# One load per chunk of keys, a product ahead of warming, second weights issued by ACT, decoding steps moved into the loop

## The chip, the cores and the metric

The kernel runs on one core of one Trainium2 chip. The metric is the device time in microseconds of one execution. The engines are PE (matrix products), DVE, ACT and POOL (elementwise work); SP only issues DMAs. SP, ACT and POOL each issue DMAs from their own instruction stream: an issue that waits holds up every instruction behind it on that engine.

## The reference

Three layers, one behind the other, on 2 sequences of 768 tokens, all in float32:

```python
for t in range(S):                                  # delta rule, 2 x 8 heads of 48
    y[:, :, t] = einsum('bhd,bhde->bhe', q[:, :, t], state)
    v_old = einsum('bhde,bhd->bhe', state, k_n[:, :, t])
    state += b[t] * outer(k_n[:, :, t], v[:, :, t] - v_old)
...
e = argmax(logits) if s == 0 or local_gate < 0.5 else previous e      # 8 experts, 384 -> 1024 -> 384
out[b, s] = p[e] * (relu(x[b, s] @ w1[e]) @ w2[e])
...
h = relu(x @ w_in); gate = sigmoid(conv over 3 tokens of h); result = (h * gate) @ w_out
```

## The kernel before, in words

**Attention.** The tokens are cut into 12 chunks of 64, six pairs of chunks. For each chunk `load_kq,c` brings keys and queries into rows 0 to 47 (heads of the first half) and 64 to 111 (second half) of one tile; rows 48 to 63 stay unused. `gram,c` multiplies keys with keys and queries on PE into one of two PSUM tiles `g`, `gev,c` (ACT, line 406) and `mev,c` (DVE, line 401) copy the result out, after which the next `gram` may use that tile. For each pair a triangular system is solved in steps `d,g,j` (lines 555 and 557; `g` numbers the system, and chunks 0 and 1 are system 0, 2 and 3 are system 1, while chunks 4 to 7 make the wide system 2, steps `dw`). System 0 is solved on POOL, behind `n5,0` (line 540), which needs `n3,0` on DVE and so stands behind `gev,5` on ACT and `mev,5` on DVE; system 1 is solved on DVE. `x2,0` (line 567) on DVE follows on the last step of system 0 and, in DVE's order, on `d,1,0`. The products `pp`, `jt`, `m1`, `m2` then build the pair's inverse; `ipv` (line 611) copies the product of `pp` out. `warm,s,n` are `n` products whose result nobody reads. The whole order is one string of words, `ORDER`; each engine takes its own instructions of it in that order.

**Experts.** At the end of attention the routing (`route1` to `route4`) finds each token's slot, POOL scatters the rows to the DRAM tensor `xs` (line 231), and `place` builds the first expert's input on PE (line 245). `Moe.start` loads the first expert's weights in four pieces (`load(0, 0..3)`: two of `w1`, two of `w2`, 768 KB each), `conv` splits a piece into two parts (ACT line 822, DVE line 823), and `split` does so for the input (ACT line 922). Each expert then runs 72 products `ph` (line 886) and 48 products `py` (line 903). From the second expert on, its input comes from `xs` by the load `xe` (line 835) and is transposed on PE (line 847).

**Last layer.** `moe2` runs 16 steps (sequence, block of 128 columns). `gemm1` (line 1096) is copied out by ACT (line 1097), `conv` (lines 1103 to 1105), `gate` and `gsplit` alternate between ACT and DVE, and `gemm2` (line 1130) sums up. `extra()` is one decoding step of the last two blocks of `w_out` (lines 996 to 1006), which `gemm2` needs only in steps 6 and 7. The loop over the steps begins after a ramp in which six steps' `gemm1` have been started.

DMAs that SP and ACT issue signal on eight semaphores, `DMAHW0` to `DMAHW7`; an issue waits until the DMA that used its semaphore before has landed.

Of the kernel before, what the change touches and what calls it, by code (L numbers as in the profile page):

```python
# [18 lines left out]
D = 48  # L19
# [259 lines left out]
class Attention:  # L279
# [76 lines left out]

    def load_kq(self, c):
        self.KQ[c] = self.kqp.tile([128, 2, 4, 2, 64], F32, name="kq", tag="kq", k=c)
        for e in range(2):
            (self.nc.scalar if e and c < 8 else self.nc.sync).dma_start(out=self.KQ[c][64 * e:64 * e + D], in_=self.kq[c, e])  # L360

    def load_v(self, p):
        self.V[p] = self.natp.tile([128, 2, 8, DV], F32, name="vn", tag="vn", k=p)
# [6 lines left out]
    def load_c(self):  # L370
        self.nc.scalar.dma_start(out=self.bt, in_=self.beta)
        self.nc.scalar.dma_start(out=self.btw, in_=self.betaw)
        self.nc.sync.dma_start(out=self.wgt, in_=self.wgb)

    def load_vt(self, p):
        self.VT[p] = self.vtp.tile([96, 2, 4, 128], F32, name="vt", tag="vt", k=p)
# [343 lines left out]
    def my(self, c, s):  # L720
        y = self.g[s][:, :, 0:4 * DV].rearrange("p e (i n) -> p e i n", i=4)
        for i in range(4):
# [4 lines left out]
                                          start=(c == 0 and i == 0), stop=True, skip_group_check=True)  # L727


ORDER = ("load_kq,0 load_kq,1 consts load_kq,4 load_kq,5 load_kq,2 load_kq,3 load_kq,6 load_c load_kq,7 load_k,0 "  # L730
# [41 lines left out]
def attention(A, R, ys):  # L772
# [4 lines left out]
                  r4=lambda k, s: R.route4(k, A.bank(s)), hot=lambda c, e: R.hot(A.gp, c, e), place=lambda c: R.place(A.sps, c), rc=R.consts, cx=R.clear_x, cy=lambda k: R.clear_y(ys, k))  # L777
    for w in ORDER.split():
        n, *a = w.split(",")
# [3 lines left out]
class Moe:  # L783
# [13 lines left out]
        self.pp = pool("m_p", 2)  # L797
        self.R, self.W, self.X, self.H = {}, {}, {}, {}

    def load(self, e, k):  # L800

        if e >= NE:
            return
        t = self.raw.tile([128, 1536], F32, name="raw", tag="raw")
        if k < 2:
            v = t.rearrange("p (k f) -> p k f", k=3)
            self.nc.sync.dma_start(out=v, in_=self.w1[e, :, 512 * k:512 * k + 512].rearrange("(k p) f -> p k f", p=128))
        else:
            g = k - 2
            v = t.rearrange("p (k d) -> p k d", k=4)  # L810
            self.nc.sync.dma_start(out=v, in_=self.w2[e, 512 * g:512 * g + 512, :].rearrange("(k p) d -> p k d", p=128))
        self.R[e, k] = v

    def conv(self, e, k):
        if e >= NE:
            return
        nc = self.nc
        p, sh = (self.w1p, [128, 3, 512]) if k < 2 else (self.w2p, [128, 4, DM])
        h = p.tile(sh, F32R, name="wh", tag="wh")
        l = p.tile(sh, F32R, name="wl", tag="wl")  # L820
        r = self.R.pop((e, k))
        nc.scalar.copy(out=h, in_=r)  # L822
        nc.vector.tensor_tensor(out=l, in0=r, in1=h.bitcast(F32), op=ALU.subtract)  # L823
        self.W[e, k] = (h, l)
        self.load(e + 1, k)
# [97 lines left out]
            self.nc.vector.tensor_tensor(out=l[:, c], in0=p, in1=h[:, c].bitcast(F32), op=ALU.subtract)  # L923

    def start(self, ctx, w, done):
        for k in range(2):
            self.load(0, k)
        for k in range(2, 4):
            self.load(0, k)
        self.conv(0, 0)  # L930
        self.split(w)
        for e in (1, 0):
            self.loadx(e)
        self.conv(0, 1)
        done()
        self.pt, self.ph, self.py = (ctx.enter_context(self.tc.tile_pool(name=n, bufs=k, space=PSUM)) for n, k in (("m_pt", 2), ("m_ph", 3), ("m_py", 3)))
        self.trx(0)
# [108 lines left out]
def moe2(ctx, tc, W, ys, idn, out, wm, decode):  # L1046
    nc = tc.nc
# [3 lines left out]
    extra = lambda: next(dec, None) if dec else None  # L1051
# [7 lines left out]
    def bank():  # L1059

        if ramp:
            p, t = ramp.pop(0)
            ramp.append((p, t))
        else:
            p, t = pa, "npt"
        return p.tile([128, 384], F32, name=t, tag=t)
# [5 lines left out]
    def xtr(b, tb):  # L1072
        if tb == 0:
            XT[b] = [xp.tile([128, 3, S], F32R, name=f"nx{b}{j}") for j in range(2)]
        x = XR.pop((b, tb))
        p = bank().rearrange("p (k t) -> p k t", k=3)
        for k in range(3):
            nc.tensor.transpose(out=p[:, k], in_=x[:, 128 * k:128 * k + 128], identity=idn)
        h, l = XT[b]
        s = slice(128 * tb, 128 * tb + 128)  # L1080
        nc.scalar.copy(out=h[:, :, s], in_=p)
        nc.vector.tensor_tensor(out=l[:, :, s], in0=p, in1=h[:, :, s].bitcast(F32), op=ALU.subtract)

    def gemm1(b, f, c, n=2):

        if c == 0:
            H[b, f] = HB[(8 * b + f) % 7]
        h = H[b, f]
        wh, wl = W["inn"]
        xh, xl = XT[b]  # L1090
        fs = slice(128 * f, 128 * f + 128)
        w = S // n
        p = bank()[:, 0:w]
        cs = slice(w * c, w * c + w)
        for j, (k, (a, x)) in enumerate((k, ax) for k in range(3) for ax in ((wh, xh), (wh, xl), (wl, xh))):
            nc.tensor.matmul(out=p, lhsT=a[:, k, fs], rhs=x[:, k, cs], start=(j == 0), stop=(j == 8))  # L1096
        nc.scalar.activation(out=h[:, 1 + w * c:1 + w + w * c], in_=p, func=AF.Relu)  # L1097

    def conv(b, f):
        h = H[b, f]  # L1100
        c = C[b, f] = hp.tile([128, S], F32, name="nc", tag="nc", bufs=5)
        cw = W["conv"]
        nc.scalar.activation(out=c, in_=h[:, 0:S], func=AF.Copy, scale=cw[:, f, 0:1])
        nc.vector.scalar_tensor_tensor(out=c, in0=h[:, 1:S + 1], scalar=cw[:, f, 1:2], in1=c, op0=ALU.mult, op1=ALU.add)
        nc.vector.scalar_tensor_tensor(out=c, in0=h[:, 2:S + 2], scalar=cw[:, f, 2:3], in1=c, op0=ALU.mult, op1=ALU.add)

    def gate(b, f):
        h, c = H.pop((b, f)), C.pop((b, f))
        nc.scalar.activation(out=c, in_=c, func=AF.Sigmoid)  # L1109
        nc.vector.tensor_tensor(out=c, in0=c, in1=h[:, 1:S + 1], op=ALU.mult)  # L1110
        G[b, f] = c

    def gsplit(b, f):
        c = G.pop((b, f))
        gh = hp.tile([128, S], F32R, name="ngh", tag="ngh", bufs=3)
        gl = hp.tile([128, S], F32R, name="ngl", tag="ngl", bufs=3)
        nc.scalar.copy(out=gh, in_=c)
        nc.vector.tensor_tensor(out=gl, in0=c, in1=gh.bitcast(F32), op=ALU.subtract)
        GT[b, f] = (gh, gl)

    def gemm2(b, f):
        if f == 0:
            for t in range(6):
                O[b, t] = po.tile([128, DM], F32, name=f"no{t}", tag=f"no{t}")
        gh, gl = GT.pop((b, f))
        wh, wl = W["out"]
        for t in range(6):
            ts = slice(128 * t, 128 * t + 128)
            for j, (a, w) in enumerate(((gh, wh), (gl, wh), (gh, wl))):
                nc.tensor.matmul(out=O[b, t], lhsT=a[:, ts], rhs=w[:, f], start=(f == 0 and j == 0), stop=(f == 7 and j == 2))  # L1130

    def fin(b):
        for t in range(6):
            o = hp.tile([128, DM], F32, name="nout", tag="nout", bufs=6)
            (nc.scalar.copy if t % 2 == 0 else nc.vector.tensor_copy)(out=o, in_=O.pop((b, t)))
            r0 = b * S + t * 128
            nc.sync.dma_start(out=out[r0:r0 + 128, :], in_=o)
# [17 lines left out]
    for c in range(2):  # L1155
        for f in range(3):
# [2 lines left out]
                xtr(0, 2 * c + f + 2)  # L1159
            if (c, f) == (0, 1):  # L1160
                extra()
    extra()
    extra()
    extra()
    gemm1(0, 0, 2, 3)
    conv(0, 0)
    gemm1(0, 1, 2, 3)
    gemm1(0, 2, 2, 3)
    gemm1(0, 3, 0)
    xtr(1, 0)  # L1170
    gate(0, 0)
    conv(0, 1)
    gemm1(0, 3, 1)
    xtr(1, 1)
# [8 lines left out]
    for i, s in enumerate(steps):  # L1183
        near, far = (steps[i + n] if i + n < len(steps) else None for n in (2, 5))
        if far:
            gemm1(*far, 0)
        if near:
            gate(*near)
        if i + 1 < len(steps):
            gsplit(*steps[i + 1])  # L1190
        if far:
            gemm1(*far, 1)
        if i in (1, 2):
            xtr(1, i + 2)
        if i + 4 < len(steps):
            conv(*steps[i + 4])
        gemm2(*s)
        if i == 2:
            xtr(1, 5)
        if s[1] == 7:  # L1200
            fin(s[0])

# [148 lines left out]
```

## Time and profile before

| | |
|---|---|
| time, median of 3 runs | 455.54 us (454.3 to 455.74) |
| the profiled execution's own time | 458.59 us |
| its span in the profile | 456.9 us |
| PE busy | 397.1 us (87%) |
| DVE, ACT, POOL busy | 296.7, 203.5, 125.0 us |
| chain that ended last, by engine | PE 74%, DVE 10%, ACT 5%, issue 4%, DMA 4% |
| mean granted TensorE clock | 0.886 of full speed |

The profiled execution is 3.05 us above the median of the runs, and its span is 1.7 us below its time. The three layers lie at about 0 to 188 us, 188 to 337 us and 337 to 457 us.

### The profile page before, as it was taken

To read this page: it belongs to the slowest core of one execution; us is meant where nothing else is said; L and a number is where in the kernel's file an instruction comes from. 1 tells how busy PE (TensorE), PEld (TensorE's weight loads), DVE (VectorE), ACT (ScalarE), POOL (GpSimd) and SP (SyncE) were. 2 spreads that over 40 slices of the span, in tenths; PEclk is the share of its full clock that TensorE was granted. 3 is DMA by queue.
4 is the path that set the end of the run, shared out by engine and by line. 5 is a ranking of instruction groups with operands and counts; after the bars stand their busy time and mean duration, and the time that the engine had idled before them with its cause. 6 is when DMAs were issued, how large, how long until landed. Compare 5 with 4: busy or idle time off the path is not lost.

```text
span 456.9 us, 13270 instructions
## 1 busy us (share of the span) xinstructions
PE 397.1 (87%) x5779; PEld 359.9 (79%) x5802; DVE 296.7 (65%) x532; ACT 203.5 (45%) x344; POOL 125.0 (27%) x260
## 2 busy tenths in 40 slices
PE   5676658868769688899999999999999799999994
PEld 3633347647657567789999999999979799999993
DVE  2666982561563115489777999999916976567671
ACT  1531221634422122177564665665435846446641
POOL 7073888482710802402022021120220000000000
PEclk9577865985986579799999999999999999999997
DMA  8949482530101215769968876972054000002003
GB/s 199 230 153 324 148 278 80 141 114 4 39 4 38 109 37 180 235 211 335 382 228 302 262 266 241 292 260 107 36 162 150 1 0 1 0 2 103 1 1 110
DMA packets 34273, 65.84 MB, mean 144 GB/s; under 512 B 3392, under 2 KB 21664, under 8 KB 34208
## 3 DMA queue, kind: packets, MB, share of 16 engines
q1 hardware_dynamic: 31040, 56.90, 39.3%
q0 software_dynamic: 1792, 5.56, 3.1%
q10 hardware_dynamic: 1376, 2.46, 2.2%
q8 instruction: 47, 0.77, 0.7%
q14 instruction: 18, 0.15, 0.1%
HBM read 49.05 MB, written 15.86 MB: 142 GB/s over the span
## 4 chain that ended last, share of the span: by engine, by line
PE 74%; DVE 10%; ACT 5%; issue 4%; DMA 4%; SPq 0%; ACTq 0%; DVEq 0%
PE ph L886 15%; PE py L903 15%; PE no L1130 11%; PE npt L1096 8%; PE sps L245 3%; PE g L352 3%; DMA kq<-in_kq_dram 2%; DMA xs<-zt 2%; PE W L671 2%; PE g L619 2%; PE g L643 2%; PE g L658 1%; DVE X L557 1%; DVE tm L555 1%; PE g L726 1%
## 5 line engine op out<-in xcount | busy, mean ns | idle before, releaser
L823 DVE TENSOR_TENSOR wl<-raw,wh 128x1536 fp32r<-128x1536 f32 x32 | 56.1, 1753 | 4.3 <-ACT wh L822 3.5
L915 POOL DMA_INDIRECT ys<-y,oi x16 | 25.8, 1613 | 119.8 <-ACT y L912 114.4
L886 PE MATMUL ph<-xh,wh 128*128 128x256 f32 x192 | 54.7, 285 | 0.8 <-ACT xh L922 0.8
L886 PE MATMUL ph<-xl,wh 128*128 128x256 f32 x192 | 54.4, 283 | 0.2 <-DVE xl L923 0.2
L886 PE MATMUL ph<-xh,wl 128*128 128x256 f32 x192 | 54.4, 283 | 0.0
L1130 PE MATMUL no<-wout,ngh 128*128 128x384 f32 x192 | 51.5, 340 | 0.0
L822 ACT CAST wh<-raw 128x1536 fp32r<-128x1536 f32 x32 | 47.2, 1475 | 0.3 <-DMA raw<-in_w_dram 0.3
L1096 PE MATMUL npt<-nx,win 128*128 128x384 f32 (+1 forms) x225 | 42.2, 340 | 2.5 <-ACT nh L1097 2.5
L903 PE MATMUL py<-wh,hh 128*128 128x384 f32 x128 | 43.6, 341 | 0.0
L903 PE MATMUL py<-wh,hl 128*128 128x384 f32 x128 | 43.1, 337 | 0.0
L903 PE MATMUL py<-wl,hh 128*128 128x384 f32 x128 | 43.0, 336 | 0.0
L1096 PEld LDWEIGHTS npt<-nx,win 128*128 128x128 f32 x225 | 39.4, 193 | 3.1 <-ACT nh L1097 2.8
L886 PEld LDWEIGHTS ph<-xh,wh 128*128 128x128 f32 x192 | 36.8, 192 | 1.5 <-ACT xh L922 1.3
L886 PEld LDWEIGHTS ph<-xl,wh 128*128 128x128 f32 x192 | 36.8, 192 | 0.4 <-DVE xl L923 0.4
L886 PEld LDWEIGHTS ph<-xh,wl 128*128 128x128 f32 x192 | 36.8, 192 | 0.0
L1130 PEld LDWEIGHTS no<-wout,ngh 128*128 128x128 f32 x192 | 35.2, 188 | 0.0
L1130 PE MATMUL no<-wout,ngl 128*128 128x384 f32 x96 | 32.5, 339 | 0.0
L352 PE MATMUL g<-wm 128*128 128x512 bf16 x65 | 25.8, 500 | 5.4 <-issue 1.5
L1110 DVE TENSOR_TENSOR nc<-nc,nh 128x768 f32<-128x768 f32 x16 | 15.3, 957 | 21.0 <-ACT nc L1109 21.0
L386 PE MATMUL g<-kq 48*64 48x128 f32 x192 | 17.8, 335 | 8.7 <-DVE M L401 8.7
L1097 ACT ACTIVATE nh<-npt 128x384 f32<-128x384 f32 (+1 forms) x25 | 12.0, 485 | 29.9 <-PE npt L1096 29.9
L903 PEld LDWEIGHTS py<-wh,hl 128*128 128x128 f32 x128 | 24.1, 188 | 0.3 <-DVE hl L890 0.3
(234 smaller groups left out, 882.3 us busy)
## 6 DMA issues: line engine op xcount, KB each, us to landing
raw<-in_w_dram SPq DMA_DIRECT2D x32, 768.0 KB, 6.8
xs<-zt SPq DMA_DIRECT2D x4, 786.0 KB, 14.1
kq<-in_kq_dram SPq DMA_DIRECT2D x16, 192.0 KB, 5.0
raw<-in_win_dram SPq DMA_DIRECT2D x6, 512.0 KB, 6.9
raw<-in_wout_dram SPq DMA_DIRECT2D x8, 384.0 KB, 6.0
xe<-xs SPq DMA_DIRECT2D x7, 393.0 KB, 6.2
vn<-in_vn_dram SPq DMA_DIRECT2D x6, 456.0 KB
kn<-in_kn_dram SPq DMA_DIRECT2D x6, 384.0 KB
```

The source lines that it names most:

```text
L245: self.nc.tensor.matmul(out=w[:, b, HCAP * k:HCAP * k + HCAP], lhsT=self.x[r, c // 2, c % 2, 128 * k:128 * k + 128], rhs=self.OH[c // 8][r ...
L352: self.nc.tensor.matmul(out=w, lhsT=self.wm[:, 0:128], rhs=self.wm, start=True, stop=True)
L386: mm(out=t[r, 0, i].rearrange("p w t -> p (w t)"), lhsT=k[:, 0], rhs=k.rearrange("p w t -> p (w t)"), start=True, stop=True)
L822: nc.scalar.copy(out=h, in_=r)
L823: nc.vector.tensor_tensor(out=l, in0=r, in1=h.bitcast(F32), op=ALU.subtract)
L886: nc.tensor.matmul(out=p[:, j].rearrange("p (c t) -> p c t", c=2), lhsT=a[:, k, fs], rhs=c[:, k], start=(n == 0), stop=(n == 8))
L903: nc.tensor.matmul(out=self.Y[c], lhsT=a[:, j, ts], rhs=w[:, f], start=(f2 == 0 and j == 0 and n == 0), stop=(f2 == 3 and j == 1 and n == 2))
L915: nc.gpsimd.indirect_dma_start(out=self.views[c][e], out_offset=bass.IndirectOffsetOnAxis(ap=I[:, c:c + 1].bitcast(U32), axis=0), in_=y, i ...
L1096: nc.tensor.matmul(out=p, lhsT=a[:, k, fs], rhs=x[:, k, cs], start=(j == 0), stop=(j == 8))
L1097: nc.scalar.activation(out=h[:, 1 + w * c:1 + w + w * c], in_=p, func=AF.Relu)
L1110: nc.vector.tensor_tensor(out=c, in0=c, in1=h[:, 1:S + 1], op=ALU.mult)
L1130: nc.tensor.matmul(out=O[b, t], lhsT=a[:, ts], rhs=w[:, f], start=(f == 0 and j == 0), stop=(f == 7 and j == 2))
```

## The change

Four edits:

1. Keys and queries of a chunk come in one load of 112 rows (0 to 111), which writes zeros into rows 48 to 63; 448 KB in place of two loads of 192 KB. All are issued by SP, where ACT issued the second half of chunks 0 to 7. The three small loads of `load_c` are all issued by ACT, first of all.
2. `ipv,0` is written directly behind `pp,0` in `ORDER`, ahead of five warming products that write the same PSUM tile.
3. The two `w2` pieces of the first expert are issued by ACT, behind ACT's half of the first `conv`; they were issued by SP directly behind the `w1` pieces.
4. Three decoding steps, ahead of the last third of `gemm1` in the ramp, go behind steps 1, 2 and 3 of the loop.

```diff
     def load_kq(self, c):
-        for e in range(2):
-            (self.nc.scalar if e and c < 8 else self.nc.sync).dma_start(out=self.KQ[c][64 * e:64 * e + D], in_=self.kq[c, e])
+        self.nc.sync.dma_start(out=self.KQ[c][0:64 + D], in_=self.kq[c])
...
-        self.nc.sync.dma_start(out=self.wgt, in_=self.wgb)
+        self.nc.scalar.dma_start(out=self.wgt, in_=self.wgb)
...
-ORDER = ("load_kq,0 load_kq,1 consts load_kq,4 load_kq,5 load_kq,2 load_kq,3 load_kq,6 load_c load_kq,7 load_k,0 "
+ORDER = ("load_kq,0 load_c load_kq,1 consts load_kq,4 load_kq,5 load_kq,2 load_kq,3 load_kq,6 load_kq,7 load_k,0 "
...
-         "seev,0,2,s nw,2 vwev,0,1,s pp,0,2 load_vt,2 vwc,1,0,s warm,3,1 vhat,0 vwt,1,0 warm,3,4 vwev,1,0,s load_k,3 "
-         "ipv,0,2 sqw,2 vhat,1 d,1,1,v jt,0,0 n3w,2 warm,2,10 load_k,2 fad,0,0 n5w,2,g jte,0,v tn,0 load_v,3 n4w,2 "
+         "seev,0,2,s nw,2 vwev,0,1,s pp,0,2 ipv,0,2 load_vt,2 vwc,1,0,s warm,3,1 vhat,0 vwt,1,0 warm,3,4 vwev,1,0,s "
+         "load_k,3 sqw,2 vhat,1 d,1,1,v jt,0,0 n3w,2 warm,2,10 load_k,2 fad,0,0 n5w,2,g jte,0,v tn,0 load_v,3 n4w,2 "
...
+    def conv(self, e, k, then=None):
         nc.scalar.copy(out=h, in_=r)
+        if then:
+            then()
         nc.vector.tensor_tensor(out=l, in0=r, in1=h.bitcast(F32), op=ALU.subtract)
...
         for k in range(2):
             self.load(0, k)
-        for k in range(2, 4):
-            self.load(0, k)
-        self.conv(0, 0)
+        self.conv(0, 0, lambda: [self.load(0, k, nc.scalar) for k in range(2, 4)])
...
-    extra()
-    extra()
-    extra()
     gemm1(0, 0, 2, 3)
...
         gemm2(*s)
+        if i in (1, 2, 3):
+            extra()
```

ACT's stream at the start of the program, before. `kq`, `bt` and `btw` are load targets, and the first COPY is `gev,0`.

```order
L360 DMA kq<-in_kq_dram 48x1024 x2
L323 ACT_TABLE_LOAD
L323 ACTIVATE warm_128<-warm_128 1x1 [waits DVE_49]
L360 DMA kq<-in_kq_dram 48x1024 x2
L360 DMA kq<-in_kq_dram 48x1024 [waits DMAHW1_49]
L360 DMA kq<-in_kq_dram 48x1024 [waits DMAHW3_49]
L360 DMA kq<-in_kq_dram 48x1024 [waits DMAHW5_49]
L371 DMA bt<-in_beta_dram 128x96 [waits DMAHW0_49]
L372 DMA btw<-in_betaw_dram 128x96 [waits DMAHW1_49]
L360 DMA kq<-in_kq_dram 48x1024 [waits DMAHW3_49]
L406 COPY G<-g_123 128x512 [waits PE_49]
```

And with the change, the same place:

```order
L370 DMA bt<-in_beta_dram 128x96
L371 DMA btw<-in_betaw_dram 128x96
L372 DMA wgt<-in_wgb_dram 96x128
L323 ACT_TABLE_LOAD
L323 ACTIVATE warm_128<-warm_128 1x1 [waits DVE_49]
L405 COPY G<-g_123 128x512 [waits PE_49]
```

The six issues with a wait on another DMA are gone from ahead of `gev,0`.

ACT's stream where the experts begin, before: the copy `ak` of the routing, the first `conv`'s copy `wh`, the input's two copies `xh`, and the copies `wh` and `hh` behind them.

```order
L197 COPY ak<-g_124 16x256 [waits DVE_49,PE_49]
L822 CAST wh<-raw 128x1536 [waits DMAHW4_49,DMAHW7_49,DMAHW2_49,Pool_49]
L922 CAST xh<-sps 128x384 [waits DVE_49,PE_49,Pool_49]
L922 CAST xh<-sps 128x384 [waits DVE_49]
L822 CAST wh<-raw 128x1536 [waits DMAHW0_49]
L889 ACTIVATE hh<-ph 128x512 [waits PE_49,Activation_49]
L822 CAST wh<-raw 128x1536 [waits DMAHW2_49]
```

And with the change:

```order
L197 COPY ak<-g_124 16x256 [waits DVE_49,PE_49]
L821 CAST wh<-raw 128x1536 [waits DMAHW3_49,DMAHW7_49,DMAHW0_49,Pool_49]
L810 DMA raw<-in_w_dram 128x4x384 [waits DMAHW7_49]
L810 DMA raw<-in_w_dram 128x4x384 [waits DMAHW0_49]
L923 CAST xh<-sps 128x384 [waits DVE_49,PE_49,Pool_49]
L923 CAST xh<-sps 128x384 [waits DVE_49]
L821 CAST wh<-raw 128x1536 [waits DMAHW4_49]
```

Two issues stand between the first `wh` and the input's copies; they wait on semaphores on which the `wh` ahead of them waits too.

ACT's stream in the ramp of the last layer, before: decoding (lines 996 and 1005), copies of `gemm1` (line 1097) and the first `conv` (line 1103).

```order
L1097 ACTIVATE nh_4925<-no_5086 128x256 [waits PE_49]
L996 ACTIVATE M_5099<-raw_4958 128x384 [waits DMAHW5_49]
L1005 CAST wout_3104<-M_5036 128x384 [waits DVE_49]
L1005 CAST wout_3104<-M_5099 128x384 [waits DVE_49]
L1097 ACTIVATE nh_4923<-no_5110 128x256 [waits PE_49]
L1103 ACTIVATE nc<-nh_4923,convw 128x768 [waits Activation_49,Pool_49]
```

And with the change:

```order
L1097 ACTIVATE nh_4913<-no_5074 128x256 [waits PE_49]
L1097 ACTIVATE nh_4911<-no_5085 128x256 [waits PE_49]
L1103 ACTIVATE nc<-nh_4911,convw 128x768 [waits Activation_49,Pool_49]
L1097 ACTIVATE nh_4912<-no_5100 128x256 [waits PE_49]
L1097 ACTIVATE nh_4913<-npt 128x256 [waits PE_49]
```

The three decoding instructions between the copies of `gemm1` are gone from the ramp; with them go eight of DVE. On every engine the order of all other instructions is as before; edit 2 moves no instruction on any engine, only waits: `ipv,0` waits for `pp,0` alone, and the first warming product behind `pp,0` waits for `ipv,0`.

## Rows read from the trace of the kernel before

**Rows 1.** Chain of waits in order of time, the start: start us, us, what.
```profile
13.26 0.44 ACTq L360
```

**Rows 2.** Timeline by engine, 13 to 35 us: start us, us, instruction, idle before and releaser.
```profile
13.74 1.07 ACT L406 COPY G<-g 128x512 f32<-128x512 f32 x2 [10.50 <-issue]
...
18.98 0.59 ACT L406 COPY G<-g 128x512 f32<-128x512 f32 x1 [0.71 <-PE g L390]
...
28.23 0.59 ACT L406 COPY G<-g 128x512 f32<-128x512 f32 x1 [2.98 <-PE g L390]
...
15.19 0.47 PE L386 MATMUL g<-kq 48*64 48x128 f32 x1 [7.43 <-DVE M L401]
...
22.13 0.64 POOL L540 TENSOR_TENSOR N<-N,X 128x256 f32<-128x256 f32 x1 [11.85 <-DVE mu L545]
...
32.75 0.18 DVE L557 TENSOR_TENSOR X<-X,tm 128x15 f32<-128x15 f32 x1
34.10 0.78 DVE L567 TENSOR_SCALAR X<-X,hs 128x256 f32<-128x256 f32 x2 [1.16 <-POOL X L557]
```

**Rows 3.** Stretches of 5 us: busy by engine, granted clock, DMA share, GB/s.
```profile
0.00:5.00 5.00, 3.74 (x10) 1.34 (x10) 2.83 (x11) 1.49 (x2) 3.67 (x23) 1.00 0.63 159
5.00:10.00 5.00, 2.76 (x98) 2.18 (x96) 0.00 (x0) 0.00 (x0) 4.10 (x22) 1.00 1.03 224
10.00:15.00 5.00, 0.00 (x0) 0.00 (x0) 0.56 (x1) 1.22 (x3) 0.28 (x1) 0.67 1.06 217
15.00:20.00 5.00, 4.81 (x136) 4.82 (x140) 3.94 (x7) 3.07 (x6) 0.00 (x0) 0.50 1.05 232
20.00:25.00 5.00, 3.52 (x116) 3.15 (x109) 4.66 (x13) 3.17 (x7) 2.40 (x7) 0.80 1.02 321
```

**Rows 4.** Timeline by engine, 42 to 45 us.
```profile
42.72 0.42 DVE L611 TENSOR_TENSOR IP<-g,nh 128x256 f32<-128x256 f32 x1 [3.14 <-PE g L352]
...
43.29 1.12 PE L619 MATMUL g<-DB,IP 32*64 32x16 f32 x64 [0.68 <-DVE tm L555]
...
44.68 1.97 POOL L454 TENSOR_TENSOR Nw<-Nw,Xw 128x1024 f32<-128x1024 f32 x1 [1.57 <-DVE Xw L446]
```

**Rows 5.** Timeline by engine, 178 to 205 us; the last row is a stretch.
```profile
184.09 0.36 ACT L197 COPY ak<-g 16x256 f32<-16x256 f32 x1 [6.17 <-remote]
...
178.32 2.28 PE L245 MATMUL sps<-G,x 64*128 64x128 f32 x36
180.72 0.61 PE L194 MATMUL g<-sel,T 128*16 128x64 f32 x8
...
188.26 5.02 PE L245 MATMUL sps<-G,x 64*128 64x128 f32 x48
...
204.22 0.82 PE L847 MATMUL pt<-idn,xe 128*128 128x128 f32 x6
...
198.21 0.37 SPq L835 DMA_DIRECT2D xe<-xs  x1
...
180.00:185.00 5.00, 4.05 (x53) 3.19 (x50) 1.77 (x9) 0.92 (x2) 4.03 (x5) 1.00 1.03 362
```

**Rows 6.** DMA issues of the page: count, KB each, median us to landing.
```profile
xe<-xs SPq DMA_DIRECT2D x7, 393.0 KB, 6.2
```

**Rows 7.** Timeline by engine, 352 to 380 us; the last three rows are the chain's.
```profile
352.89 0.38 ACT L1097 ACTIVATE nh<-no 128x256 f32<-128x256 f32 x1
...
363.07 0.51 ACT L1097 ACTIVATE nh<-npt 128x384 f32<-128x384 f32 x1
...
363.64 3.23 PE L1096 MATMUL npt<-nx,win 128*128 128x384 f32 x9 [2.52 <-ACT nh L1097]
...
379.59 0.96 DVE L1110 TENSOR_TENSOR nc<-nc,nh 128x768 f32<-128x768 f32 x1 [2.19 <-ACT nc L1109]
...
343.80 1.04 PE no L1096 x9
...
348.99 0.48 DVE S L1000
...
376.74 3.12 PE npt L1096 x18
```

More of the change, by code (lines that the diff above doesn't have):

```diff
@@ L798, in __init__, with load @@
         self.R, self.W, self.X, self.H = {}, {}, {}, {}
-    def load(self, e, k):
+    def load(self, e, k, eng=None):
         if e >= NE:
@@ L810, in load @@
             v = t.rearrange("p (k d) -> p k d", k=4)
-            self.nc.sync.dma_start(out=v, in_=self.w2[e, 512 * g:512 * g + 512, :].rearrange("(k p) d -> p k d", p=128))
+            (eng or self.nc.sync).dma_start(out=v, in_=self.w2[e, 512 * g:512 * g + 512, :].rearrange("(k p) d -> p k d", p=128))
         self.R[e, k] = v
-    def conv(self, e, k):
+    def conv(self, e, k, then=None):
         if e >= NE:
@@ L925, in start @@
     def start(self, ctx, w, done):
+        nc = self.nc
         for k in range(2):
             self.load(0, k)
-        for k in range(2, 4):
-            self.load(0, k)
-        self.conv(0, 0)
+        self.conv(0, 0, lambda: [self.load(0, k, nc.scalar) for k in range(2, 4)])
         self.split(w)
@@ L1326 @@
     arrays = {
-        "in_kq_dram": np.ascontiguousarray(kq.reshape(12, 2, 48, 2, 4, 2, 64)),
+        "in_kq_dram": np.concatenate([kq.reshape(12, 2, 48, 1024), np.zeros((12, 2, 16, 1024), np.float32)], axis=2).reshape(12, 128, 2, 4, 2, 64)[:, 0:112].copy(),
         "in_kn_dram": np.ascontiguousarray(kn.reshape(6, 128, 2, 8, 48)),
```

## The prediction
> **What bounds the kernel now.** I read the chain of waits first, by stage. From the first product of the experts to the last product PE hardly ever waits, so only the seams count: the start, the passage from attention to the experts, and the ramp of the last layer. In attention the chain runs through ACT, DVE and POOL in turn, so there the timeline by engine has to be read for what each engine waits for last. The table of stretches then gives the rate of the DMAs and the granted clock.
>
> At the start ACT does nothing for 10.50 us before `gev,0` at 13.74 us [rows 2]. The label "issue" names no releaser. The chain shows what it is: ACT's last load issue stands right ahead, at 13.26 us [rows 1], and by the program six of ACT's issues wait for earlier DMAs to land. PE waits 7.43 us behind it, for DVE's `mev`, which waits for ACT [rows 2]. All of attention hangs on this: POOL begins the first system (`n5,0`) at 22.13 us after 11.85 us of idling, and DVE goes on with `x2,0` at 34.10 us, released by POOL [rows 2].
>
> At the passage, ACT copies `ak` at 184.09 us, though PE's product for it ran from 180.72 to 181.33 us, and the label "remote" names no engine; in that stretch the DMAs are busy in full (share 1.03, 362 GB/s) with the 3 MB of first weights [rows 5]. Everything behind it is late: the last 48 products of `place` end at 193.28 us, and they run at half the pace (48 in 5.02 us, against 36 in 2.28 us) [rows 5].
>
> In the ramp of the last layer, the chain leaves PE: from 348.99 us it goes through decoding on DVE and ACT, the copy of `gemm1` that stands behind decoding comes at 352.89 us, and PE waits 2.52 us at 361.12 us for a later copy of that stream [rows 7].
>
> **Edit 1, the loads.** It removes six blocked issues from ACT. Its own three issues wait for nothing, so `gev,0` follows `gram,0`; what comes late next are the loads themselves. A chunk now moves 458,752 bytes instead of 393,216, and 0.15 MB of small loads go ahead. The stretches add up to 0.80, 1.92, 3.00, 4.16 and 5.77 MB at 5, 10, 15, 20 and 25 us [rows 3]. On that curve chunk 5, the fourth loaded, is there after 1.99 MB, at 10.3 us, and chunk 7, the last, after 3.82 MB, at 18.5 us. Two `gram`s took from 15.19 to 18.98 us at a clock of 0.50 [rows 2, 3], 1.9 us each, so 0.95 us at full clock. `gram,5` then ends at 11.3 to 12.2 us. `gev,5` to `n5,0` is 22.13 - 18.98 = 3.15 us [rows 2], so POOL begins at 14.4 to 15.4 us, 6.7 to 7.7 us earlier. The other thing `x2,0` stands behind, `d,1,0`, ended 32.93 - 28.23 = 4.7 us after `gram,7` [rows 2]: now 18.5 + 1.9 + 4.7 = 25.1 us, while POOL ends at 34.10 - 7.0 = 27.1 us. POOL still comes last. **Term: 7.0 us.** Bounds: at 159 GB/s from the start chunk 5 lands at 12.5 us and the gain is 4.6; at 321 GB/s [rows 3], from 1.9 us on (0.63 of the first stretch was busy), at 8.1 us and 9.9.
>
> The curve was made by two queues, and now one carries all. From 20 to 25 us only SP's loads were moving, and that is the fastest row, 321 GB/s [rows 3]. The Trainium skill (DMA: Bandwidth & Descriptors, "Issuing engines are not separate DMA queues") says that DMAs issued by different engines run on the same 16 DMA engines, so one queue or two would move the same; by it the term stays 7.0, and if a single queue were slower it would be the last rival's. The trace agrees with the page as far as that row goes.
>
> **Edit 2, `ipv`.** `ipv,0` waited 3.14 us for warming products and began at 42.72 us; `jt`, behind them on PE, at 43.29 us after waiting 0.68 [rows 4]. Moved, `ipv` runs about 2.7 us earlier, but PE's first warming product now waits its 0.42 us, and `jt` still stands behind all five: 0.68 back, 0.42 and a hand-over paid. POOL's `n5w` waited 1.57 us for DVE [rows 4] and can begin that much earlier, but then its steps run beside those of DVE's system 1 at larger sizes. I take 0, bounds -0.5 and +1.6. Its cover is PE's warming; without it the edit would be worth the 0.68 us.
>
> **Edit 3, second weights.** Half of the 3 MB leaves the stretch before 185 us, and comes behind ACT's first `wh`. If that frees ACT's `ak`, it gains 184.09 - 181.33 = 2.76 us; if PE also keeps its clock, 48 products cost 48/36 x 2.28 = 3.04 instead of 5.02 us, 1.98 more: upper bound 4.7 us. Against it: `xe` of the second expert was issued at 198.21 us, waiting for POOL's scatters; 6.2 us to landing [rows 6] make 204.4 us, and PE transposes it at 204.22 us [rows 5]. There is no slack, so the gain is only as large as the scatter's, and the 1.5 MB, 4.2 us at 362 GB/s, now move just ahead of the last scatters. I take 2.0; below, no help for ACT and a scatter delayed by a third of 4.2 us: -1.5. ACT's two issues hide in its wait for `place`, and the second weights are first copied behind the first of the expert's products.
>
> **Edit 4, decoding.** The copy at 352.89 us needs nine products that begin behind DVE's work at 348.99 and last 1.04 us [rows 7]: it can run at 350.1. I replayed ACT's and DVE's stream from there with the durations that each kind has; the 2.8 us shrink where ACT meets products that PE has not finished, and the copy PE waits for comes 1.6 us earlier than 363.07 [rows 7]. PE's gap falls from 2.5 to 0.9 us. Behind the gap nine products took 3.23 us; at full clock nine take 1.56 [rows 7], so another 1.7 us come back if the clock holds. I take 2.5, between 1.6 and 3.3. The decoding lands behind steps whose pace PE sets and where DVE idles 2.19 us a step [rows 7]; the largest moved piece is four operations of about half a microsecond. Without that idle time it would cost those 2 us once, still off PE's path.
>
> **Sum.** 7.0 + 0 + 2.0 + 2.5 = 11.5 us: 458.6 becomes 447.1 for the profiled execution, which lies 3.05 us above the median; so 455.5 becomes **444.0 us**.
>
> **Rivals.**
> 1. *Attention gives half of it back* (waits for instructions, POOL and DVE in each other's way): 3.5 + 2.0 + 2.5 = 8.0, 447.5 us. For it: PE and ACT have idle times without a releaser. Against it: nothing between 13 and 62 us in the chain waits for a load.
> 2. *The second weights collide with the scatter*, term -1.5: 7.0 - 1.5 + 2.5 = 8.0, 447.5 us. It decides as soon as `xe` is issued later relative to the last `place`.
> 3. *All bounds good*: 9.0 + 4.7 + 3.3 = 17, 438.5 us.
> 4. *Both 1 and 2*: 4.5, 451.0 us.
> 5. *Slower: one load of 112 rows uses fewer DMA engines.* With 7 of 16, 224 GB/s [rows 3] become 98; chunk 7 lands at 39.0 us, `d,1,0` ends at 45.6 and `x2,0` is 11.5 us late: 455.5 + 11.5 - 4.5 = 462.5 us. The whole is a loss below about 119 GB/s, where chunk 7 lands at 32.0 us and `x2,0` is 4.5 us late. Against it stands the slowest full stretch, 217 GB/s [rows 3], and nothing for it. The Trainium skill (same page, "Why a DMA increments its semaphore by 16 and not by 1") states that the number of engines is the largest up to 16 that divides the slowest dimension; 112 gives 16, which would rule this rival out; no run here shows it yet.
> That ACT stays blocked is excluded: the order shows no wait on a DMA ahead of `gev,0`.
>
> **Chances.** Forecast 45%, rival 1 17%, rival 2 18%, rival 3 9%, rival 4 6%, rival 5 4%, no change 1%. About 0.3% (1.4 us) is what a measurement can tell: faster 0.94, same 0.02, slower 0.04. The range 438.5 to 449.5 us takes in rivals 1 to 3 and leaves out 4, 5 and some of the tails; the forecast's own is 440.5 to 447.
>
> **What would show it.** `gev,0` at about 6.5 us; `n5,0` at 14 to 16; `x2,0` at 26 to 28; the last chunk of eight landed by 20. `ak` less than 1 us behind its product, `xe` at most 7 us ahead of PE's transposes without a wait there. PE's gap in the ramp under 1.2 us. The prediction is wrong if DVE's `x2,0` is early but the last `place` is not, or if PE waits for `xe`.

## The result: 1% faster, less than half of what was forecast

The changed kernel takes 454.33 us (median of 20 runs, 445.72 to 459.52), the kernel before on the same chip 458.56 us (20 runs, 451.0 to 465.56): 4.2 us less, ratio 0.9899 with a 95% interval of 0.9855 to 0.9942. The forecast was 11.5 us less. Single runs of one kernel spread over some 14 us, so ratios are formed from the quicker runs of both kernels. Each trace below is of one execution, so its times carry that spread. The profiled execution took 454.96 us, its span is 453.3 us at a mean granted clock of 0.885.

**The start came nearly as forecast.** Timeline by engine, 6 to 29 us, of the changed kernel:

```profile
6.50 0.59 ACT L405 COPY G<-g 128x512 f32<-128x512 f32 x1 [2.77 <-PE g L389]
...
24.38 0.59 ACT L405 COPY G<-g 128x512 f32<-128x512 f32 x1 [4.49 <-PE g L389]
...
14.94 0.64 POOL L539 TENSOR_TENSOR N<-N,X 128x256 f32<-128x256 f32 x1 [4.66 <-DVE mu L544]
...
26.62 0.22 POOL L556 TENSOR_TENSOR X<-X,tm 128x15 f32<-128x15 f32 x1
...
28.55 0.18 DVE L556 TENSOR_TENSOR X<-X,tm 128x15 f32<-128x15 f32 x1
28.64 0.77 DVE L566 TENSOR_SCALAR X<-X,hs 128x256 f32<-128x256 f32 x2
...
14.47 0.37 PE L389 MATMUL g<-kq 48*64 48x64 f32 x2 [1.81 <-issue]
...
22.34 0.37 PE L389 MATMUL g<-kq 48*64 48x64 f32 x2 [2.73 <-issue]
```

`gev,0` stands at 6.50 us instead of 13.74, POOL begins 7.2 us earlier [rows 2], `x2,0` 5.5 us. POOL is done at 26.84 us, but `x2,0` has to wait for `d,1,0` on DVE (28.55 + 0.18): PE waited twice, 1.81 and 2.73 us, for nothing that the profile shows, and `gram,7` came late: `gev,7` waits 4.49 us for it and begins at 24.38 us, where the prediction has `gram,7` done at 20.4. The loads were not at fault for these two waits: loads_only, the kernel before with edit 1 alone, has the same two (1.92 and 2.45 us, at 14.68 and 22.27 us), and in its trace the eighth chunk had landed at 17.27 us. Stretches of 5 us (busy by engine, granted clock, DMA share, GB/s), against [rows 3]:

```profile
0.00:5.00 5.00, 3.75 (x10) 1.27 (x10) 2.83 (x11) 1.49 (x2) 3.67 (x23) 1.00 0.58 164
5.00:10.00 5.00, 3.50 (x145) 3.08 (x144) 1.89 (x3) 2.41 (x4) 4.10 (x22) 1.00 1.05 295
10.00:15.00 5.00, 2.37 (x86) 2.02 (x87) 4.69 (x12) 2.41 (x5) 0.34 (x2) 0.95 1.04 298
15.00:20.00 5.00, 4.61 (x120) 4.21 (x114) 2.99 (x6) 2.89 (x5) 4.06 (x13) 0.50 1.05 278
```

One queue moved 278 to 298 GB/s; 7 of 16 DMA engines would have given the 98 of the last rival. By the Trainium skill (DMA: Bandwidth & Descriptors, "Issuing engines are not separate DMA queues") DMAs run on the same 16 DMA engines whichever engine issues them; these rows agree.

**The middle gave the start back, in this execution.** The results of `r,1` to `r,11` (called first to eleventh R; DVE, line 675) are good milestones. Timeline of DVE, changed kernel:

```profile
61.08 0.63 DVE L675 TENSOR_TENSOR R<-vn,W 128x456 f32<-128x456 f32 x1 [0.52 <-PE W L670]
...
127.98 0.63 DVE L675 TENSOR_TENSOR R<-vn,W 128x456 f32<-128x456 f32 x1 [1.08 <-PE W L670]
...
176.50 0.63 DVE L675 TENSOR_TENSOR R<-vn,W 128x456 f32<-128x456 f32 x1 [0.19 <-PE W L670]
```

Before they stood at 67.32, 127.19 and 174.50 us: 6.2 us early, then 0.8 and 2.0 us late. Stretches of 10 us of the changed kernel show PE as the engine with hardly any time left, at half clock (1.2 GHz) from 60 us into the third row:

```profile
60.00:70.00 10.00, 9.34 (x294) 7.57 (x296) 3.56 (x8) 1.43 (x4) 8.90 (x15) 0.50 0.50 160
70.00:80.00 10.00, 10.00 (x274) 7.97 (x273) 1.73 (x4) 3.55 (x6) 6.74 (x18) 0.50 0.31 82
80.00:90.00 10.00, 9.22 (x324) 6.06 (x317) 5.85 (x15) 4.87 (x13) 2.75 (x3) 0.86 0.34 95
```

The stretch from the first R to the seventh says what was lost, first the kernel before, then the changed one:

```profile
67.32:127.19 59.87, 48.72 (x1791) 39.19 (x1802) 27.25 (x61) 22.10 (x49) 39.43 (x95) 0.78 0.27 73
61.08:127.98 66.90, 56.97 (x1802) 42.84 (x1802) 26.98 (x61) 22.27 (x49) 40.27 (x98) 0.68 0.25 70
```

PE is busy for 8.25 us more, but busy time times granted clock, as an estimate of the work at full clock, is 38.0 and 38.7 us: it is the same work at a lower clock. PE's waits here are small in both: 4.0 and 3.5 us for other engines, 6.0 us in each without a releaser.

**The passage and the ramp.** Timeline by engine, 182 to 204 us and 360 us, changed kernel, against [rows 5, 7]:

```profile
182.72 0.61 PE L194 MATMUL g<-sel,T 128*16 128x64 f32 x8
...
188.77 2.95 PE L245 MATMUL sps<-G,x 64*128 64x128 f32 x48
...
193.45 0.39 PE L887 MATMUL ph<-xh,wh 128*128 128x256 f32 x1 [0.76 <-ACT xh L923]
...
202.66 0.82 PE L848 MATMUL pt<-idn,xe 128*128 128x128 f32 x6
...
185.19 0.36 ACT L197 COPY ak<-g 16x256 f32<-16x256 f32 x1 [5.27 <-DMA xall<-x]
...
360.64 1.83 PE L1096 MATMUL npt<-nx,win 128*128 128x384 f32 x9 [1.00 <-ACT nh L1097]
```

`ak` is still 1.86 us behind its product. The 48 products of `place` run in 2.95 us instead of 5.02, PE does not wait for `xe`, and its gap in the ramp is 1.00 us instead of 2.52.

### The profile page after: what moved, and what is told of

The parts are those of the page before. It is cut to its first block, busy times and chain, and to the rows that moved or that the text cites. A ratio compares the mean times of both kernels' runs of the same rounds, so it can differ in the third digit from the quotient of the medians.

```text
span 453.3 us, 13281 instructions
## 1 busy us (share of the span) xinstructions
PE 402.3 (89%) x5802; PEld 358.9 (79%) x5802; DVE 297.7 (66%) x532; ACT 203.6 (45%) x344; POOL 124.8 (28%) x260
## 4 chain that ended last, share of the span: by engine, by line
PE 79%; DVE 10%; issue 4%; ACT 3%; DMA 1%; SPq 0%; DVEq 0%; ACTq 0%
PE ph L887 15%; PE py L904 15%; PE no L1130 11%; PE npt L1096 8%; PE g L352 4%; PE no L1096 3%; PE sps L245 2%; PE W L670 2%; PE g L657 2%; PE g L618 2%; PE g L642 2%; PE g L725 2%; PE g L385 2%; DVE X L556 2%; DVE tm L554 1%
## 5 line engine op out<-in xcount | busy, mean ns | idle before, releaser
L1096 PE MATMUL npt<-nx,win 128*128 128x384 f32 (+1 forms) x225 | 40.7, 332 | 1.0 <-ACT nh L1097 1.0
L1096 PEld LDWEIGHTS npt<-nx,win 128*128 128x128 f32 x225 | 38.1, 188 | 1.5 <-ACT nh L1097 1.3
L887 PEld LDWEIGHTS ph<-xh,wh 128*128 128x128 f32 x192 | 36.8, 192 | 1.5 <-ACT xh L923 1.3
L887 PEld LDWEIGHTS ph<-xl,wh 128*128 128x128 f32 x192 | 36.8, 192 | 0.4 <-DVE xl L924 0.4
L887 PEld LDWEIGHTS ph<-xh,wl 128*128 128x128 f32 x192 | 36.8, 192 | 0.0
L352 PE MATMUL g<-wm 128*128 128x512 bf16 x87 | 32.9, 500 | 3.8 <-DVE warm L305 1.3
L231 POOL DMA_INDIRECT xs<-x,IDX x12 | 13.3, 1111 | 42.3 <-DVE lp L158 23.5
```

Of the source, the lines that this page charges most:

```text
L231: nc.gpsimd.indirect_dma_start(out=self.views[tb, c], out_offset=bass.IndirectOffsetOnAxis(ap=self.IDX[:, tb, c:c + 1].bitcast(U32), axis= ...
L352: self.nc.tensor.matmul(out=w, lhsT=self.wm[:, 0:128], rhs=self.wm, start=True, stop=True)
L887: nc.tensor.matmul(out=p[:, j].rearrange("p (c t) -> p c t", c=2), lhsT=a[:, k, fs], rhs=c[:, k], start=(n == 0), stop=(n == 8))
```

## Milestones of all kernels

Taken from each kernel's timeline; the last two columns are lengths, from the first `ph` to the end of the last `py`, and from there to the end of PE's last product. "Median" is against the kernel before on the same chip. The kernels ran on different chips: loads_only, no_loads, no_w2 and no_dec on one, again, dec_only, fill_mid and fill_both on a second, w2_only, no_ipv, fill_no_w2 and before_fill on a third, no_warm on a fourth, and the last three rows on a fifth. Two single runs of 1954 and 1220 us (in no_loads and dec_only), whose cause is not known, are not counted in the fits.

| kernel | R 1 | R 7 | R 11 | first ph | experts | last layer | median |
|---|---|---|---|---|---|---|---|
| before | 67.3 | 127.2 | 174.5 | 195.0 | 141.8 | 113.3 | |
| changed | 61.1 | 128.0 | 176.5 | 193.5 | 141.7 | 110.4 | -4.2 |
| again | 61.4 | 123.0 | 170.4 | 190.7 | 141.7 | 110.3 | -5.3 |
| loads_only | 60.4 | 127.1 | 169.8 | 185.0 | 141.8 | 113.4 | -6.3 |
| no_loads | 68.5 | 127.9 | 169.2 | 185.2 | 142.7 | 110.3 | -2.6 |
| no_w2 | 62.5 | 128.1 | 170.9 | 186.3 | 141.9 | 110.2 | -6.1 |
| no_dec | 61.4 | 127.3 | 170.6 | 185.6 | 142.9 | 113.3 | -3.8 |
| dec_only | 67.3 | 130.0 | 177.7 | 198.0 | 141.7 | 110.3 | -1.6 |
| w2_only | 67.3 | 130.4 | 173.1 | 188.3 | 142.3 | 113.3 | +3.7 |
| no_ipv | 61.0 | 127.3 | 170.4 | 185.8 | 142.7 | 110.4 | -4.1 |
| fill_mid | 61.5 | 120.1 | 169.3 | 186.6 | 141.7 | 110.2 | -11.9 |
| fill_both | 61.4 | 126.4 | 173.8 | 191.3 | 142.3 | 110.5 | -9.8 |
| fill_no_w2 | 61.0 | 121.8 | 163.7 | 179.0 | 141.8 | 110.3 | -7.2 |
| before_fill | 66.9 | 128.9 | 172.2 | 187.2 | 142.1 | 113.3 | +0.6 |
| no_warm | 60.8 | 115.0 | 161.1 | 178.1 | 141.7 | 110.3 | -14.2 |
| before_no_warm | 66.8 | 122.9 | 170.6 | 187.7 | 143.2 | 113.6 | -7.7 |
| after_no_warm | 61.6 | 116.3 | 162.8 | 179.9 | 143.1 | 110.5 | -10.4 |
| mid_no_warm | 61.1 | 118.7 | 168.2 | 188.1 | 141.8 | 110.4 | -7.8 |

## Experiment 1: one edit alone, one edit less

Each kernel is the one before with only the named hunk of the diff (`_only`), or the changed one with that hunk taken back (`no_`); "again" is the changed kernel itself.

> The kernel before with edit 1 alone. Theory A (PE gives the early start back: in the changed kernel's trace POOL is 7.2 us early at 15 us, but PE's work between 60 and 130 us is granted 0.50 for longer and the last place is no earlier): x2,0 5 to 7 us earlier, the first product of the experts not more than 1.5 us earlier, and the median 0 to 1.5 us below the kernel before. Theory B (the loss in the one profiled execution is chance, the early start goes through in most runs): median 4 to 7 us below the kernel before.

> The changed kernel with edit 1 undone. Theory A: the whole measured gain comes from edits 3 and 4, so 4 to 5.5 us below the kernel before, as the changed kernel. Theory B: most of the gain is gone, 0 to 2 us below the kernel before.

> The changed kernel with edit 3 undone: the second weights are loaded with the first again. Theory A: from the last of attention (2.0 us later than before) to the first product of the experts (1.6 us earlier) the changed kernel gained 3.5 us, which are lost here: about 1 us below the kernel before. Theory B: the 3.5 us were PE's clock in that execution and not the loads' doing; then the median is within 1 us of the changed kernel's, about 4 us below the kernel before.

> The changed kernel with edit 4 undone: the decoding steps stand ahead of the last layer's products again. Theory A: the 2.1 us between the first product of the experts (1.6 us earlier) and the end (3.6 us earlier) are lost: 2 to 2.5 us below the kernel before, and PE's gap near 360 us is back at about 2.5 us. Theory B: the decoding only moved the wait; the median is within 1 us of the changed kernel's.

> The changed kernel itself, unchanged, on the chip of the other runs, as the mark against which they are read. If the edits add up, it stands about 1.6 us above the kernel without edit 3 (that edit's two stages were longer by that much) and 3 us below the kernel without edit 4: 4 to 6 us below the kernel before.

> The kernel before with edit 4 alone. By the ramp's length in the traces (113.3 us from the experts' last product to the end with the decoding ahead, 110.3 behind) 3.0 us below the kernel before, with PE's gap near 361 us gone. The rival, that decoding later slows DVE's steps and gives it back: within 1 us of the kernel before.

> The kernel before with edit 3 alone. By the theory that edit 3 is worth nothing: from the last R to the first product of the experts 15 to 17.5 us where the clock holds 1.00 there and about 20.4 where it falls to 0.5, as without the edit; the median within 1.5 us of the kernel before. By the prediction's step: 2.0 us below.

> The changed kernel with edit 2 undone. By the prediction 0 (bounds 1.6 faster to 0.5 slower with the edit): the first R behind it within 0.7 us of 61.1 to 61.5 us, the median that of the changed kernel, 4 to 6 us below the kernel before.

Measured: the medians and milestones of the table. Neither theory stands as put. In every trace with edit 1 and the warming as it was, the first R is 5 to 7 us early and the seventh is at 123 to 128 us, as theory A says; but the median of loads_only is 6.3 us lower, as theory B says. A least-squares fit over all 257 runs of all batches (one level for each chip, one term for each edit and for each kind of warming) gives, with standard errors: edit 1 -5.1 +- 0.8 us, edit 2 +0.3 +- 1.0, **edit 3 +1.5 +- 0.7**, edit 4 -1.9 +- 0.8; together -5.1 +- 0.6. It takes the edits as additive, so it sizes the terms and shows no mechanism. One run weighs in it, no_loads at 465.36 us: without it edit 1 is -4.4, edit 3 +1.3 and edit 4 -2.2. The ratio of w2_only alone is 1.0091 (1.0047 to 1.0136): slower, where 2.0 us less was forecast and no more than 1.5 us of difference by the other theory.

Of the rest, again (-5.3) and no_ipv (-4.1) came out as expected. no_loads (-2.6) and no_dec (-3.8) lie outside both of their theories, though PE's gap in the ramp of no_dec is back at 2.53 us; no_w2 (-6.1) gained 2 us more than theory B; dec_only gained 1.6 us where 3.0 was expected. The traces of loads_only, no_w2 and no_dec are of executions 4.9, 2.4 and 3.6 us above their medians and that of no_loads of one 1.5 us below, so on that chip the traces show edit 1 as worth less than the runs do.

The traces tell why edit 3 does not help. loads_only has the kernel before's order of weight loads, no_dec the new one, both on one chip. Timeline of PE and ACT, loads_only:

```profile
176.06 0.61 PE L194 MATMUL g<-sel,T 128*16 128x64 f32 x8
...
176.71 0.36 ACT L197 COPY ak<-g 16x256 f32<-16x256 f32 x1 [3.46 <-DVE G L239]
```

The same of no_dec, and its waits of PE (us in total, times, longest), 184 to 215 us:

```profile
176.78 0.61 PE L194 MATMUL g<-sel,T 128*16 128x64 f32 x8
...
177.43 0.36 ACT L197 COPY ak<-g 16x256 f32<-16x256 f32 x1 [3.45 <-DVE G L239]
```

```profile
PE ph L887 <- DVE xl L850: 0.5, 1, 0.5
PE pt L848 <- DMA xe<-xs: 0.3, 1, 0.3
```

`ak` follows its product within 0.04 us in both. In all eight traces of this chip and of the third one it does so, with edit 3 or without; in all others it is late, by 1.9 to 2.8 us (0.9 in fill_both), with edit 3 (changed, again, fill_mid, fill_both, after_no_warm) or without (before, dec_only, no_warm, before_no_warm, mid_no_warm). So the weights did not hold it. What edit 3 adds, on those two chips, is that `xe` is issued 7.3 to 7.8 us behind the end of the last `place`, against 6.8 to 7.1 without it, and that PE then waits for the second expert's input; in no_dec 0.3 us for `xe` and 0.5 us behind it. The experts' stage is 142.3 to 142.9 us long in the four traces with edit 3 there (no_loads, no_dec, w2_only, no_ipv), 141.8 to 142.1 in the four without it (loads_only, no_w2, fill_no_w2, before_fill). That is 0.2 to 1.1 us; the rest of the fit's 1.5 us, and of the 3.7 us of w2_only, is not shown.

And the 3.5 us that the changed kernel's trace shows at the passage were the clock: from the last R to the first `ph` the traces of before and dec_only (without edit 3) and again (with it) have 6.8 us at half clock and take 20.3 to 20.5 us; no_loads, no_dec, w2_only and no_ipv (with it) and loads_only, no_w2, fill_no_w2 and before_fill (without) have none and take 15.0 to 16.0. As stretches, before and loads_only (without edit 3), then again and no_dec (with it):

```profile
174.50:195.01 20.51, 17.86 (x296) 15.63 (x289) 9.79 (x37) 3.77 (x7) 7.69 (x7) 0.83 0.76 245
169.84:184.99 15.15, 13.99 (x296) 12.33 (x289) 9.84 (x37) 3.77 (x7) 7.35 (x7) 1.00 0.89 293
...
170.38:190.65 20.27, 17.73 (x295) 15.58 (x289) 9.80 (x37) 3.77 (x7) 7.57 (x7) 0.83 0.78 259
170.56:185.61 15.05, 13.89 (x297) 12.23 (x289) 9.84 (x37) 3.77 (x7) 7.36 (x7) 1.00 0.84 280
```

Edit 4 is as clear in the other direction: the last layer takes 113.3 to 113.6 us in every trace without it and 110.2 to 110.5 with it, 3.0 us.

## Experiment 2: filling PE's idle time

```diff
-"... my,0,1 sev,0,s dw,2,10,g ..."
+"... my,0,1 warm,0,12 sev,0,s dw,2,10,g ..."
```

In fill_both also `warm,3,1` behind `r1,0` becomes `warm,3,13`.

> The changed kernel with 12 warming products in PE's idle time between 54.9 and 59.3 us, which fit into it at full clock (2.8 us) and nearly at half (5.2 us). Theory A, the clock (the early start is lost because PE is granted 0.50 from 58 to 82 us while it has work all the time): the clock stays full into the sixties, the third R comes 3 to 5 us earlier than 85.4 us and the median is 2 to 4 us below the changed kernel. Theory C (PE would have to wait there for DVE, POOL or its instructions anyway; the clock only fills the wait): third R within 1 us, median within 1 us of the changed kernel or up to 1 us above it.

> As the one before, and 12 more warming products in PE's second idle time, between 132 and 138 us. Theory A: the granted clock is full from about 134 us on instead of from 141, and another 1 to 3 us come back by the last R. Theory C: no difference from the kernel before it in this list beyond 1 us.

> The changed kernel with the 12 warming products between 54.9 and 59.3 us and with edit 3 undone. If edit 3 is worth nothing or costs up to 1.6 us (the theory after the first traces: its 3.5 us in the changed kernel's trace were the clock, which was 1.00 there and 0.58 before), this is the fastest of all, 11 to 13.5 us below the kernel before. If edit 3 is worth its 2.0 us, 8 to 10 us below.

> The kernel before with the same 12 warming products, which lie there in PE's idle time between 60.9 and 65.5 us. Theory A (clock): the stretch at 0.50 from 62.6 to 79.6 us is shorter in the kernel before too, the third R comes up to 3 us before 88.2 us, and the median is 2 to 4 us lower; less than in the changed kernel, where the stretch was 24 us long. If the filling were worth nothing without the early start: within 1 us.

fill_mid did what theory A says, and more. Stretches of 10 us, fill_mid:

```profile
60.00:70.00 10.00, 8.11 (x359) 6.16 (x359) 3.87 (x8) 2.02 (x5) 8.90 (x15) 1.00 0.50 170
70.00:80.00 10.00, 6.96 (x290) 5.44 (x292) 3.42 (x5) 4.48 (x9) 7.32 (x18) 1.00 0.49 128
```

PE is busy for 15.1 us of these 20 instead of 19.3 at half clock, the third R comes at 81.80 instead of 85.44 us and the seventh at 120.08, and the median is 11.9 us below the kernel before, 6.6 below the changed kernel on the same chip (again), where 2 to 4 was expected. But in the other three traces the clock fell to 0.5 at 65 to 67 us although PE had just been filled, and their third R (85.32, 84.88 and, without edit 1, 92.09 us) lies where it does without the filling: 84.6 to 87.5 us with edit 1, 88.2 to 92.4 without. before_fill gains nothing in its median (+0.6), fill_no_w2 1.1 us over no_w2 where 5 or more was expected. The fit gives the filling -3.3 +- 1.1 us behind edit 1 and -1.4 +- 1.2 without it. Over the 14 traces with warming, one more microsecond at half clock between the second and the seventh R goes with 0.37 us more time (correlation 0.90), and from the first to the seventh R, PE's busy time times the granted clock is 36.8 to 40.3 us in all of them: the longer stretches hold the same work at a lower clock. Filling PE's idle time does not hold the clock reliably.

## Experiment 3: more warming, and none

sprinkle1 and sprinkle3, without edit 3 and with the filling of fill_mid, put one or three more products behind each of the 12 groups of small products that follow.

> The changed kernel without edit 3, with the 12 warming products in PE's idle time and one more behind each of the 12 groups of small products that follow (59 to 75 us): 0.22 us each at full clock, 2.6 us in all. In three of four traces with the 12 alone the clock still fell 5 to 9 us behind them, while PE was busy. Theory A: the larger products in between hold the clock longer, the time from the second to the seventh R is below 49 us and the median is up to 3 us below the same kernel without them (which was 7.2 us below the kernel before). Theory C (the clock is not what the stretch depends on): 1 to 3 us above it, by the added products.

> As the one before with three in each of the 12 places: 36 products, 7.8 us at full clock and 15.5 at half. Theory A: the clock holds 1.00 from 56 us to past 80, which gives back up to 12 us of PE's time for 7.8 us spent: 0 to 4 us below the kernel with the 12 alone, or even. Theory C: the added products lengthen a stretch in which PE has no slack: 6 to 12 us slower than with one in each place.

Both took 1887 us and tell nothing of the question: the added products write to a PSUM bank that `qs,1,1` has filled and `xev,1,1` has not yet read, so these two kernels compute with other data. no_warm is the changed kernel without edit 3 and without every `warm` of the order but the ten at the very start; after_no_warm and before_no_warm are the changed kernel and the one before in that way, and mid_no_warm, also without edit 3, leaves out only the 24 products from `se,1,0` to `r1,0`.

```diff
-"... warm,1,2 m1ev,1,0,s ks,2 ... vhat,2 dt,2 warm,3,6 m1ev,2,2,s ..."
+"... m1ev,1,0,s ks,2 ... vhat,2 dt,2 m1ev,2,2,s ..."
```

> The changed kernel without edit 3 and without any of attention's 77 warming products (those at the very start stay). Theory A: the mean granted clock of the run falls by 0.02 or more, half clock fills nearly all of 14 to 175 us, and the median is 3 us or more above the same kernel with them (6.1 us below the kernel before). Theory C: the products only fill waits and cost PE up to 0.5 us each where it has none: 0 to 5 us below it.

> The kernel before without attention's 77 warming products (those at the very start stay). Theory D (from the second R on PE has work all the time, so the products lie on the path: 24 of them between 59 and 128 us): 4 to 10 us below the kernel before, with the late start still there. If they bind only because the early start has moved everything onto PE: within 2 us of the kernel before, or slower.

> The changed kernel with all its edits, without the 77 products. Theory D: the early start now goes through to the end, so this is 5 us or more below the kernel before without them, and 11 to 14 us below the kernel before. Theory A, if the gain of the kernel without them lay elsewhere: not more than 3 us below the kernel before without them.

> The changed kernel without edit 3 and without only the 24 warming products between 59 and 128 us, where PE hardly waits. Theory D: R 7 at 115 to 118 us as without all 77 (115.0), not at 122 to 128 us, and 10 to 14 us below the kernel before. If the gain came from the other 53: 5 to 8 us below.

no_warm gains the most of all: 441.50 us against 455.71, ratio 0.9704 (0.9654 to 0.9754), at a lower mean granted clock (0.866 over its runs, 0.888 in the kernel before's). Theory A expected it to be slower; as the whole explanation it falls. It gains 8.1 us more than no_w2 did on another chip, beyond theory C's 5 as well. The products' own time is the other part. Stretch from 59 to 128 us of the changed kernel, the warming products alone (PE busy, PEld busy, granted clock, DMA share, GB/s):

```profile
59.00:128.00 69.00, 11.87 (x28) 2.35 (x29) 0.67 0.27 80
```

That is 11.9 of the 58.8 us for which PE is busy there. Without them the seventh R stands 13.0 us before that of the changed kernel (timeline of DVE, no_warm):

```profile
115.02 0.63 DVE L675 TENSOR_TENSOR R<-vn,W 128x456 f32<-128x456 f32 x1 [1.47 <-PE W L670]
```

Not all of this is the products' time: from the first to the seventh R, PE's busy time times the granted clock falls from 38.7 to 32.3 us, and the granted clock there is 0.72 instead of 0.68, so taking them out cost no clock in this stretch. Timeline of DVE and PE, before_no_warm:

```profile
66.83 0.63 DVE L676 TENSOR_TENSOR R<-vn,W 128x456 f32<-128x456 f32 x1 [0.52 <-PE W L671]
...
122.90 0.63 DVE L676 TENSOR_TENSOR R<-vn,W 128x456 f32<-128x456 f32 x1 [1.66 <-PE W L671]
...
187.71 0.38 PE L880 MATMUL ph<-xh,wh 128*128 128x256 f32 x1 [1.73 <-ACT xh L916]
```

and after_no_warm:

```profile
61.57 0.63 DVE L675 TENSOR_TENSOR R<-vn,W 128x456 f32<-128x456 f32 x1 [0.54 <-PE W L670]
...
116.28 0.63 DVE L675 TENSOR_TENSOR R<-vn,W 128x456 f32<-128x456 f32 x1
...
179.92 0.38 PE L881 MATMUL ph<-xh,wh 128*128 128x256 f32 x1 [1.73 <-ACT xh L917]
```

Here the early start goes through: 5.3 us at the first R, 6.6 at the seventh, 7.8 at the first product of the experts. The medians of the two differ by 2.7 us only (the means by 4.1), where 5 or more was expected, so the traces are the better case; that is open. Theory D stands for the kernel before (-7.7 us, 4 to 10 expected), and misses its place: mid_no_warm gains 1.7 us over no_w2, not 4 or more, with the seventh R at 118.73 us and half clock at the passage in its trace. Its 7.8 us below the kernel before are what was expected if the gain lay with the other 53 products; by the medians, of different chips, those count for 6.4 us.

## Why the prediction was wrong

**Edit 3 is the largest error**, 2.0 us forecast as a gain, 1.5 +- 0.7 us of loss measured. The step that failed is "If that frees ACT's `ak`, it gains 184.09 - 181.33 = 2.76 us": a wait without a named engine beside DMAs that were busy in full was put down to them. `ak` is late on some chips and not on others, whatever the weights do. Its second half, that PE also keeps its clock, 1.98 us more, failed too: the half clock at the passage comes and goes with either order of the loads. What remained was the cost on the other side, rival 2: by the sign that it named (`xe` is issued later behind the last `place`), by PE's wait for `xe`, and by its size of 1.5 us in the fit, of which the traces show 0.2 to 1.1.

**Edit 1 was over-sized**: 7.0 us forecast, 5.1 +- 0.8 measured, within its bounds of 4.6 to 9.9, though only just (4.4 without the run at 465.36 us). The working at the start was right for `gev,0` and `n5,0`; PE's two waits made DVE's `d,1,0` the last to come and not POOL, so `x2,0` began at 28.64 us and not at 27.1. What failed behind it is that the term was carried through to the end: "All of attention hangs on this" left out that PE has little time to spare from the first to the seventh R, where it waited only 4.0 us for other engines even before, and that its pace there is its clock, 0.78 before and 0.68 in the changed kernel's trace. In this pair of traces that is rival 1 by its place and not by its mechanism, since PE's waits of either kind did not grow. On the chip of loads_only PE's waits without a releaser in this stretch are 2.0 us in no_loads and 3.9 to 5.7 in the three kernels with edit 1, so a part may be rival 1's there. Why the clock was lower stays open: in the six traces with edit 1 and all the warming, without filling, it is 0.65 to 0.71, in the four without edit 1 0.69 to 0.78, so edit 1 alone does not decide it. How much of this is in the mean of many runs stays open too.

**Edit 4 was right**: 3.0 us in the traces, 2.5 forecast, PE's gap at 1.00 us with 0.9 forecast. The fit gives 1.9 +- 0.8. **Edit 2 was right**: +0.3 +- 1.0, 0 forecast; no_ipv's first R stands where the changed kernel's does.

By the fit 6.4 us are missing from the sum of 11.5: 3.5 by edit 3, 1.9 by edit 1, the rest by edits 2 and 4. It is rival 4, both losses together, 4.5 us, that came out by its number; it stood outside the range with 6%, and its half that is rival 1 came out smaller (1.9 us for 3.5) and, where the traces show it, mostly by another mechanism. The two losses were taken as mishaps independent of the forecast, but each came from the same habit: a term read at the stage where it arises and not followed through the next one.

## What to carry to other kernels

A wait that names no engine is not explained by what happens to be busy beside it; look for the same wait in another execution or on another chip before giving it a price. An earlier start is worth what the next stage's engines can spare: add up that stage's busy time with the wait gone, fillers included, and read its clock. Products that were put into waits to hold PE's clock are work like any other: here they cost the kernel before 7.7 us already, so try the kernel without them, and again after each change that moves its stages.

## What the runs showed of the hardware

The granted clock differs between runs of one kernel, and the time goes with it: of the changed kernel's 20 runs the one at 0.912 has a span of 444.0 us, the one at 0.870 has 457.8, and the correlation is -0.83.

PE was granted 0.50 from 70 to 80 us in the changed kernel while it was busy 10.00 of 10 us (above), with products of 128 and fewer columns on 32 to 64 rows and four warming ones. The Trainium skill (TensorE: Matmul & The Clock Gate, "What's actually happening") says that the gate follows how busy PE has been; these rows do not agree if busy is what the profile counts, and in three of four traces with the filling the clock fell 3.0 to 6.3 us behind its last product while PE went on working. The measurement decides: busy time in the profile does not tell the clock.

Waits for nothing that the profile shows differ from chip to chip. The same 64 products of `jt,5` in the changed kernel on one chip (timeline of PE; of nine such rows the first, the fifth and the last):

```profile
152.78 0.40 PE L618 MATMUL g<-DB,IP 32*64 32x16 f32 x5
...
155.53 0.42 PE L618 MATMUL g<-DB,IP 32*64 32x16 f32 x6 [0.32 <-issue]
...
159.12 1.05 PE L618 MATMUL g<-DB,IP 32*64 32x16 f32 x28 [1.01 <-issue]
```

and in no_w2 on another:

```profile
152.84 1.91 PE L618 MATMUL g<-DB,IP 32*64 32x16 f32 x64
```

7.4 us against 1.9. In all traces of the two chips where `ak` is on time these products take 1.1 to 1.9 us, in all traces of the others 6.4 to 8.1, whatever the edits: a difference between chips, and no part of the change. Whether `ak` is late there for the same reason is not shown.
